# Windowed attention feeding a Fourier mixing block: dilated heads of batch 0 moved into the mixing tiles by one-hot products

## The chip, the cores and the metric

The kernel runs on one core of a Trainium2 chip. The metric is the device time of one execution in microseconds (us). Five things work side by side: TensorE (PE, matrix products), VectorE (DVE), ScalarE (ACT), GpSimd (POOL), and SyncE (SP), which here only issues DMAs. TensorE writes into PSUM, whose eight banks of 512 fp32 columns are handed out by name.

## The reference

All of it is fp32. Eight batches, eight heads, 576 tokens, head width 64, model width 512, hidden width 2048.

```python
scores = (q @ k^T) / 8                    # q, k, v: [8, 8, 576, 64]
rel = pos[:, None] - pos[None, :]
heads 0..3: keep 0 <= rel < 32            # "plain"
heads 4..7: keep 0 <= rel < 128, rel % 4 == 0   # "dilated"
attn = softmax(where(keep, scores, -1e9)); x = attn @ v   # x: [8, 576, 512]
u = x + real(fft(fft(x, axis=1), axis=2))
un = (u - mean(u)) / sqrt(var(u) + 1e-6)
out = u + relu(un @ w_ch1) @ w_ch2        # [512, 2048], [2048, 512]
```

## The kernel before

**Stages.** For each batch there are eight attention units (plain or dilated, `j` = pair of heads, `u` = first or second half of the tokens), then a mixing step, then the feed-forward net of that batch's tokens. Six of the sixteen hidden blocks of the net (`NF1 = 6`) are done in a first pass, called fill (`up`, L1104, and `down`, L1120), while attention and mixing of later batches still run; the other ten are done in a late stage (L1386, L1484, L1451) that follows.

**One attention unit** (`attend`): scores by products of 64 columns of weights on quarters of the array (L636), a mask with a row maximum on DVE (L667), `exp` on ACT (L673), transposes on PE (L687), a copy of the transposed probabilities out of PSUM on ACT (L692, L697), products with `v` on PE (L723), then sums, reciprocals and a scaled eviction on DVE (L733, L735, L746, L751). fp32 products appear as two instructions each in the trace; transposes as one. Dilated heads are computed with tokens regrouped by residue modulo 4, so that they too have a plain band.

**How batch 0 gets into the mixing.** The mixing folds token t with token 576 - t, so it wants rows 0 to 288 ("plus") in the tiles x0, x2, xt0 and the mirrored rows ("minus") in x1, x3, xt1. Batch 0 does its dilated heads first: they are evicted into `xt` and `xl`, stored to DRAM by `store` in pieces (segments of constant residue) that put the tokens in order, and fetched back by the first lines of `fold`. For batch 0 both ways go through POOL's DMA queue (`Q_ST0`, `Q_X0`; L543 for all of them). The plain heads of batch 0 are then written straight into the x tiles (L740). Their second half is `straight`: its products with `v` are made by `across` (L706 to L711) with 64 columns of weights, and at four places with one column of weights, one after the other in the order of a list. Later batches store and fetch both kinds through SP's queue.

**The mixing** (`mix`): `fold` (L873 to L898), products along the sequence with the tables `seq` (L924), products along the channels with the tables `chn` (L970, L976), the sum into the x tiles (`add_u`), layer norm (`normalise`), and for batch 0 transposes on PE (`turned`, L818) into the operand of the fill. In `mix` the products along channels run over the row groups 0, 2, 1, and layer norm and transposes of group 0 follow those of group 2.

**Feed-forward weights** arrive as fp64 words and are narrowed on ACT and DVE (`narrow`, L1045 to L1056), then split into a high and a low part (`two_parts`, L1062 to L1066). In the kernel before, the first six of the twelve weight tiles of the fill have their high part copied on POOL (L1062), the rest on ACT (L1064).

**The order of the work** is made by a planner (`Plan.run`) when the program is built: every operation has an engine, a cost, a priority (a number; smaller goes first) and its dependences, and a list scheduler with a model of the engines, the PE clock and the DMAs lays each engine's instructions out in one fixed order. On the chip each engine works that order off in sequence, so an instruction whose input is late holds all that stand behind it. The constants P_... are offsets in those priorities, T_SEQ and T_CHN are earliest times in the model for the issue of the tables `seq` and `chn` on POOL's queue, NGANG is the unit from which scores wait for the eviction of two units before, and NPT2 and NAV2 say how many units use two banks rather than one for transposes and for products with `v`; one of the two banks is lent by the fill (`ff`), whose first use waits until these units are done.

**Spin products.** Up to 250 pairs of products of a blank tile (L564) are put into the order wherever PE has nothing else to do; their result is not used. They are left out from the time the model has given out the first bank to the fill or the eleventh to the mixing.

Of the kernel before, what the change touches and what calls it, by code (L numbers as in the profile page):

```python
# [18 lines left out]
C, FF = 512, 2048  # L19
# [20 lines left out]
NPT2, NAV2 = 11, 11  # L40
NGANG = 6
NHP = 6
W_ON = (("POOL", "POOL"), ("POOL", "ACT"))
# [4 lines left out]
NFD, NUD, NFL = 1, 0, 1  # L48
# [7 lines left out]
Q_ST0, Q_X0 = 'P', 'P'  # L56
# [6 lines left out]
GAP = 32  # L63
DIL = 4
# [147 lines left out]
class Plan:  # L212
# [60 lines left out]
    def run(self):  # L273
# [164 lines left out]
def fused_kernel(ctx: ExitStack, tc, qk, v, w1, w2, seq, tail, chn, alt, mask, ident, perm, flip, out):  # L438
# [98 lines left out]

    def dma(fn, r, w, prio, nbytes, slow=1):
        return add("SP", 0.5, fn, r, w, prio, nbytes * slow)
# [7 lines left out]
    def start():  # L547
# [9 lines left out]
        for t in qks + lent[:1]:  # L557
            zero(t, "POOL", 0.1, lambda t=t: nc.gpsimd.memset(t()[:, GAP - WIN:GAP], 0.0), "z", -8.0)
        zero(blank, "DVE", 0.3, lambda: nc.vector.memset(blank().bitcast(F32), 0.0), None, -9.0)
        spin = Buf(ap=mixes[0][:, NSP:NSP + 220])  # L560
        for n in range(NSPIN):
            def turn_over(n=n):
                for k in range(2):
# [5 lines left out]
        for t, p, w in ((xs[1], 0, C // 2), (xtail[1], 32, C // 2)):  # L569
            zero(t, "DVE", 0.1, lambda t=t, p=p, w=w: nc.vector.memset(t()[p:p + 1, 0:w], 0.0), "row")  # L570
# [6 lines left out]
        for b in range(B):  # L577
# [5 lines left out]
    def tables_in():  # L583
        def table(dst, src, key, prio, nbytes):
            add("POOL", 0.55, lambda: nc.gpsimd.dma_start(out=dst(), in_=src), (), (key,), prio, nbytes, at=T_SEQ if prio == P_SEQ else T_CHN)
# [13 lines left out]
    def attention(b, when):  # L599
        for n, dil in enumerate((0, 1) if b else (1, 0)):  # L600
            xts = []
            if b or dil:
                xts = [attw("xt", [P, 2, 4, D], F32, NXT) for _ in range(2)] + [attw("xl", [P, 2, D], F32, 1)]
            for j in range(2):
                attend_pair(b, dil, j, 2 * n + j, xts, lambda u: when(6 * n + 3 * j + 1.5 * u))

# [16 lines left out]
    def attend(b, dil, j, u, num, qk_, vt, xts, prio):  # L623
# [55 lines left out]
        def order(m):  # L679
            if m == 4 or not dil and m == 3:  # L680
# [32 lines left out]
        def values():  # L713
            if straight:
                across(0)
                across(1)
# [36 lines left out]
        if j == 1:  # L753
            store(b, dil, u, xt, xl, prio)

# [86 lines left out]
    def mix(b, when):  # L842
# [10 lines left out]
        def fold(m, prio):  # L853
# [3 lines left out]
            if m < 2:  # L857
                xp, xm = tiles[m]
                at = slice(0, P)
                for x, src in ((xp, plus), (xm, minus)):  # L860
                    send("S" if b else Q_X0, lambda x=x: x()[:, cs], lambda src=src: src()[P * m:P * m + P, cs],
                         (src,), ((x, 0),), early, P * (2048 if b else 1024))
            else:
# [5 lines left out]
                ):  # L869
# [25 lines left out]
            either(b < NFL, NEH, lambda on: on.tensor_tensor(  # L895
                out=hl(1, 0), in0=ee()[:n], in1=hl(0, 0).bitcast(F32), op=ALU.subtract), (ee, eb), (eb,), prio)
            either(b < NFL, 2 * P, lambda on: on.tensor_tensor(
# [161 lines left out]
    def two_parts(src, need, dst, key, n, eng, prio, high="ACT"):  # L1059

        if high == "POOL":
# [513 lines left out]
```

## Time and profile before

| | us |
|---|---|
| median of 3 runs (range) | 1024.17 (1023.91 to 1027.3) |
| the profiled execution, whole | 1026.06 |
| its span, first to last instruction | 1024.3 |
| PE busy in the span | 1010.2 (99%) |
| of it, spin products (L564) | 37.1 |
| DVE, ACT, POOL busy | 730.9, 474.1, 291.5 |
| mean granted PE clock | 0.992 |

The profile is one execution; its own time is 1.89 us above the median. "Granted clock" is the share of TensorE's full speed: 1.00 is 2.4 GHz, 0.50 is 1.2 GHz. "PEld" is the loading of weights into the array, which overlaps the products. A row of a timeline gives start, duration, engine, source line, operation, output<-inputs and, in brackets, how long the engine stood idle before and what ended that. A PE that is busy with L564 does nothing useful.

### The profile page before, as it was taken

The numbers are of one execution on the slowest core, as the hardware profiler recorded it, in microseconds if no ns is written. First come the engines' busy times: TensorE is split into PE (matmuls) and PEld (weight loads), VectorE is DVE, ScalarE is ACT, GpSimd is POOL, SyncE is SP. The second block draws the span as 40 slices with busy tenths as digits, with TensorE's granted clock in tenths as the row PEclk, the third lists the DMA queues.
The fourth block names the chain that finished last, engine by engine and source line by source line (L and its number), as shares of the span: only waits on it lengthen the run. The fifth ranks groups of instructions, "written<-read, shape, count | busy, mean of one in ns | idle before, by whom it ended". The sixth has DMA issues, their size and how long they took to land.

```text
span 1024.3 us, 22200 instructions
## 1 busy us (share of the span) xinstructions
PE 1010.2 (99%) x8371; PEld 902.1 (88%) x8371; DVE 730.9 (71%) x2151; ACT 474.1 (46%) x1180; POOL 291.5 (28%) x353
## 2 busy tenths in 40 slices
PE   9999899999999999999999999999999999999998
PEld 8788688888988988899998898989898989898987
DVE  4489987878766687877575476858585858585846
ACT  5365756655645343434434443526252625262522
POOL 3536572536434557441321010101010101010200
PEclk9799999999999999999999999999999999999999
DMA  9867778786763545234354132323232323232221
GB/s 291 256 201 233 243 205 225 225 233 181 228 180 104 159 122 170 86 115 144 124 155 104 52 83 83 83 83 83 83 83 83 84 83 83 83 84 83 83 62 42
DMA packets 98875, 137.91 MB, mean 135 GB/s; under 512 B 9678, under 2 KB 62143, under 8 KB 98768
## 3 DMA queue, kind: packets, MB, share of 16 engines
q1 hardware_dynamic: 94112, 125.66, 42.1%
q0 software_dynamic: 4128, 9.71, 3.4%
q8 instruction: 66, 1.08, 0.5%
q10 hardware_dynamic: 528, 1.11, 0.3%
q14 instruction: 41, 0.34, 0.1%
HBM read 99.24 MB, written 37.21 MB: 133 GB/s over the span
## 4 chain that ended last, share of the span: by engine, by line
PE 88%; DVE 5%; DMA 4%; ACT 1%; issue 1%; SPq 0%; POOL 0%; DVEq 0%; ACTq 0%; POOLq 0%
PE bank L1386 24%; PE bank L1484 20%; PE bank L1120 13%; PE bank L1104 12%; PE bank L723 3%; PE bank L970 3%; PE bank L636 3%; PE bank L687 3%; PE bank L924 3%; DMA seq<-in_seq_dram 2%; PE bank L564 2%; PE bank L1451 1%; PE bank L709 1%; DVE pm L667 1%; DMA wst<-in_w_dram 1%
## 5 line engine op out<-in xcount | busy, mean ns | idle before, releaser
L1386 PE MATMUL bank<-low,wb 128*128 128x512 f32 x1080 | 255.6, 389 | 0.0
L1386 PEld LDWEIGHTS bank<-low,wb 128*128 128x128 f32 x1080 | 198.0, 188 | 36.9
L1104 PE MATMUL bank<-ut,low 128*128 128x256 f32 x1296 | 167.1, 282 | 0.8 <-DVE low L1112 0.8
L1104 PEld LDWEIGHTS bank<-ut,low 128*128 128x128 f32 x1296 | 157.1, 189 | 3.8 <-DVE low L1112 1.2
L1120 PE MATMUL bank<-low 128*128 128x512 f32 x648 | 156.4, 392 | 0.5 <-DVE low L1112 0.5
L1148 POOL DMA_INDIRECT ut<-us,flip_sb x20 | 41.7, 2083 | 393.2 <-DVE ut L1205 208.5
L1120 PEld LDWEIGHTS bank<-low 128*128 128x128 f32 x648 | 118.6, 188 | 23.8 <-DVE low L1112 0.7
L1392 ACT ACTIVATE xa<-bank 128x256 f32<-128x256 f32 x90 | 34.2, 380 | 176.6 <-PE bank L1386 176.6
L673 ACT ACTIVATE pm<-pm,mx 128x96 f32<-128x96 f32 x256 | 83.1, 369 | 55.4 <-DVE mx L667 54.4
L1423 DVE TENSOR_TENSOR y<-xa 128x384 f32<-128x384 f32 x45 | 25.1, 558 | 101.9 <-ACT xa L1392 101.6
L1112 DVE SCALAR_TENSOR_TENSOR low<-bank,low 128x256 fp32r<-128x256 f32 x108 | 45.2, 420 | 49.4 <-ACT low L1110 48.7
L1110 ACT ACTIVATE low<-bank 128x256 fp32r<-128x256 f32 x108 | 41.1, 382 | 72.9 <-PE bank L1104 72.2
L1194 DVE TENSOR_TENSOR ut<-ut,bank 128x512 f32<-128x512 f32 (+1 forms) x136 | 73.1, 547 | 2.1
L1227 DVE STREAM_TRANSPOSE ut<-ut 128x512 f32<-128x512 f32 (+1 forms) x76 | 70.2, 976 | 5.1 <-DMA ut<-us 5.0
L1484 PEld LDWEIGHTS bank<-w2s,low 128*128 128x128 f32 x588 | 71.7, 188 | 2.1
L1484 PE MATMUL bank<-w2s,low 128*128 128x256 f32 x588 | 72.1, 278 | 0.0
L667 DVE CUSTOM_DVE_ANT_0 pm<-bank,mask_sb 128x96 f32<-128x96 f32 x256 | 54.7, 249 | 18.6 <-PE bank L636 17.7
L1484 PEld LDWEIGHTS bank<-w2s,hm 128*128 128x128 f32 x483 | 58.9, 188 | 1.8
L1484 PE MATMUL bank<-w2s,hm 128*128 128x256 f32 x483 | 59.2, 278 | 0.0
L1140 ACT COPY row<-bank 128x512 f32<-128x512 f32 x36 | 21.1, 585 | 78.0 <-PE bank L1120 67.8
L1064 ACT CAST low<-y 128x640 fp32r<-128x640 f32 (+1 forms) x50 | 35.8, 716 | 41.2 <-DVE y L1425 23.9
L1484 PE MATMUL bank<-low 128*128 128x256 f32 x420 | 51.5, 278 | 0.0
(187 smaller groups left out, 1810.1 us busy)
## 6 DMA issues: line engine op xcount, KB each, us to landing
qk<-in_qk_dram SPq DMA_DIRECT2D x30, 576.0 KB
vt<-in_v_dram SPq DMA_DIRECT2D x31, 438.8 KB
us<-uc SPq DMA_DIRECT2D x36, 257.0 KB
part<-row SPq DMA_DIRECT2D x36, 256.0 KB
wst<-in_w_dram SPq DMA_DIRECT2D x18, 512.0 KB
ut<-us SPq DMA_DIRECT2D x36, 256.0 KB
ut<-part SPq DMA_DIRECT2D x36, 256.0 KB
ut<-us SPq DMA_DIRECT2D x64, 128.0 KB
```

The source lines that it names most:

```text
L667: nc.vector.tensor_tensor_reduce(prob(i)[ps_], sc()[e][ps_, KB * (i // 2):KB * (i // 2) + KB], mask_sb().bitcast(F32)[ps_, kind], -0.125, ...
L673: add("ACT", 0.265, lambda i=i: nc.scalar.activation(out=prob(i), in_=prob(i), func=AF.Exp, bias=mx()[:, i:i + 1], scale=-1.0), ((mx, i),) ...
L1064: add("ACT", act(n), lambda: nc.scalar.copy(out=dst(0), in_=src()), need, ((key[0], (key[1], 0)),), prio)
L1104: nc.tensor.matmul(z()[:, :n_tok], lhsT=wf()[a][:, kk], rhs=ut()[:, p, kk], start=(kk == 0 and n == 0), stop=(kk == KT - 1 and n == 2),)
L1110: add("ACT", act(n_tok) - 0.05, lambda: nc.scalar.activation(out=h()[:, 0, :n_tok], in_=z()[:, :n_tok], func=AF.Relu), (z,), ((h, 0),), prio)
L1112: add("DVE", dve(n_tok), lambda: nc.vector.scalar_tensor_tensor(h()[:, 1, :n_tok], z()[:, :n_tok], 0.0, h()[:, 0, :n_tok].bitcast(F32), op ...
L1120: nc.tensor.matmul(acc(), lhsT=h()[:, a, P * s:P * s + P], rhs=wf()[:, p], start=(first and n == 0), stop=(last and n == 2),)
L1148: add("POOL", 1.04, lambda: nc.gpsimd.indirect_dma_start(dst(), None, us[idx // 4](), bass.IndirectOffsetOnAxis(ap=flip_sb()[:, 4 * kk + i ...
L1194: add("DVE", dve(C if at in (outer, inner) else TOK1), lambda: nc.vector.tensor_tensor(out=blocks(part())[:, at], in0=blocks(part())[:, at ...
L1227: nc.vector.transpose(out=o[back], in_=x[:, g])
L1386: nc.tensor.matmul(z(), lhsT=wb1[NF1 + 2 * p + f]()[:, a, kk], rhs=ut()[:, x, kk], start=(kk == 0 and n == 0), stop=(kk == KT - 1 and n == 2),
L1484: nc.tensor.matmul(acc()[block // 2][:, TOK1 * (block % 2):TOK1 * (block % 2) + TOK1], lhsT=part(hl, a, i, i + 1), rhs=w2s[p]()[:, j, x], ...
```

## The change

- **Dilated heads of batch 0.** They no longer go through DRAM. A tile `comb` holds two identity patterns spread over every fourth column; slices of it are one-hot matrices. After each dilated unit, `settle` multiplies such slices with the evicted `xt` and `xl` (fp32) into a bank of PSUM called home, which puts the tokens in order and separates plus from minus; `settled` copies home into the x tiles (six copies of 256 columns on ACT, and one memset on POOL). There are three homes (row groups 0, 1, 2), taken from the two banks of the mixing. `store` and the fetch in `fold` are left out for batch 0, and so is the zero row of its `xsm`. The transposes of the dilated units of batch 0 use the plain identity instead of `perm`.
- **One-column products.** `across` issues all twelve products with 64 columns of weights of both heads first and the eight with one column last.
- **Order in `mix`.** The products along channels of all three row groups are listed before any layer norm and transposes; the banks of the mixing are given out in that order.
- **Spin products.** 32 columns instead of 220, into another bank, and left out only once the fill has its first bank.
- **Weights.** The high parts of all twelve weight tiles of the fill are copied on ACT.
- **Constants.** T_SEQ and T_CHN are gone, NPT2 and NAV2 go from 11 to 13, NGANG from 6 to 10, and all priority offsets differ. NFL is replaced by NFD of the same value; Q_ST0 and Q_X0 are no longer used.

```diff
-NPT2, NAV2 = 11, 11
-NGANG = 6
-NHP = 6
-W_ON = (("POOL", "POOL"), ("POOL", "ACT"))
+NPT2, NAV2 = 13, 13
+NGANG = 10
-P_QK0, P_V0 = -8.77, -8.57
-P_ST, P_FD, P_WD, P_ST0, P_FD0, P_SPAN0, P_SPAN1 = 6.01, -1.43, -0.9, -38.42, -6.42, 14.09, 37.25
-P_QK, P_V, P_TR, P_MIX, P_SPAN, P_W, P_WF, P_FILL, P_FILLT = 7.55, 24.08, -5.32, 2.19, 23.68, 14, 4.61, 45.36, 4.44
-P_MIX0, P_MIX1 = -4.08, -39.02
-P_SEQ, P_CHN = -11.04, -19.08
-T_SEQ, T_CHN = 4.31, 37.98
+P_QK0, P_V0 = -3.77, -0.7
+P_ST, P_FD, P_WD, P_ST0, P_FD0, P_SPAN0, P_SPAN1 = -9.42, -1.79, -5.67, -44.72, -26.2, -0.04, 23.28
+P_QK, P_V, P_TR, P_MIX, P_SPAN, P_W, P_WF, P_FILL, P_FILLT = 3.24, 3.62, -16.9, 1.77, 11.53, 21.01, 4.61, 39.84, 3.58
+P_MIX0, P_MIX1 = 8.6, -13.7
+P_SEQ, P_CHN = -30.6, 12.62
+P_HOME = 7.4
+BACK = 4 * P + 72
-            if o.prio == SPIN and (turn["ff"] or turn["mix"] > 10):
+            if o.prio == SPIN and turn["ff"]:
+    comb = work("y1", [P, 2, 2, NSP], F32R, 1)
+    def teeth(lo, n):
+        return comb().rearrange("p a c k -> p (a c k)").bitcast(F32)[:, lo:lo + n]
+        zero(comb, "DVE", 0.8, lambda: nc.vector.memset(teeth(0, 4 * NSP), 0.0), None, -9.0)
+        for k in range(2):
+            add("DVE", 0.2, lambda k=k: nc.vector.tensor_copy(
+                out=teeth(k * BACK, 4 * P)[:, ::4], in_=ident_sb().bitcast(F32)[:, k]), (ident_sb,), (comb,), -8.0)
-        spin = Buf(ap=mixes[0][:, NSP:NSP + 220])
+        spin = Buf(ap=pair[0][:, 5 * KB:512])
-                    nc.tensor.matmul(spin(), lhsT=blank(), rhs=blank().unsqueeze(1).broadcast_to([P, 2, P])[:, :, 0:110],
-                                     start=n + k == 0, stop=True, skip_group_check=True)
+                    nc.tensor.matmul(spin(), lhsT=blank(), rhs=blank()[:, 0:32], start=True, stop=True)
...
         def order(m):
+            if dil and not b:
+                return ident_sb().bitcast(F32)[:, 0], 0
...
-        def across(e):
-            for k, g, lo, n, t in ((0, 0, 0, QB, 8), (0, 1, 64, QB, 7), (0, 1, 64, 1, 8), (2, 0, 128, QB, 6), (2, 0, 128, 1, 7),
-                                   (2, 1, 192, QB, 5), (2, 1, 192, 1, 6), (4, 0, 256, QB, 4), (4, 0, 256, 1, 5), (4, 1, 289, QB, 4)):
+        def across():
+            for e, (k, g, lo, n, t) in itertools.chain(itertools.product(range(2), (
+                    (0, 0, 0, QB, 8), (0, 1, 64, QB, 7), (2, 0, 128, QB, 6), (2, 1, 192, QB, 5), (4, 0, 256, QB, 4), (4, 1, 289, QB, 4))),
+                    itertools.product(range(2), ((0, 1, 64, 1, 8), (2, 0, 128, 1, 7), (2, 1, 192, 1, 6), (4, 0, 256, 1, 5)))):
...
-        if j == 1:
+        if b and j == 1:
             store(b, dil, u, xt, xl, prio)
+    def settle(m, j, u, xts, home, prio):
+        xt, xl = xts[u], xts[2]
+        n = (P, P, 33)[m]
+        todo = [(0, r, P * r, xt, r % 2) for r in (2 * u, 2 * u + 1)]
+        rows = P if m < 2 else 32
+        for s_ in (2 * u, 2 * u + 1):
+            for r in range(4):
+                lo, hi = max(P * s_, 144 * r + (112, 80, 72)[m]), min(P * s_ + P, 144 * r + (144, 112 + (r == 0), 80 + (r == 0))[m])
+                if lo < hi:
+                    todo.append((1, r, P * s_, xt, s_ % 2))
+        if u and m < 2:
+            todo += [(1, 3, 4 * P - QB * e, xl, e) for e in range(2)]
+        def go(side_):
+            for k, (side, r, first, src, at) in enumerate(todo):
+                if side != side_:
+                    continue
+                off = 575 * r - 4 * first
+                lhs = teeth(BACK + 4 * P - 4 - (off + S - P * m), rows) if side else teeth(off + P * m, n)
+                o = home()[:rows if side else n, 256 * side:256 * side + 256].rearrange("p (e h d) -> p h e d", e=2, h=2)[:, j]
+                o, x = (o[:, at], src()[:, j]) if src is xl else (o, src()[:, at, j::2, :])
+                nc.tensor.matmul(o, lhsT=lhs, rhs=x, start=k == 0 and not j and not u, stop=True, skip_group_check=True)
+        for side in range(2):
+            add("PE", 0.215 * sum(t[0] == side for t in todo), lambda side=side: go(side), ((xt, j), comb) + ((xl, j),) * u * side, (home,), prio)
+    def settled(m, home, prio):
+        for side, x in enumerate(xtail if m == 2 else xs[2 * m:2 * m + 2]):
+            n = P if m < 2 else 33 - side
+            add("ACT", act(C // 2) - 0.05, lambda x=x, side=side, n=n: nc.scalar.copy(
+                out=x()[:n, C // 2:C], in_=home()[:n, 256 * side:256 * side + 256]), (home,), ((x, "dil"),), prio)
...
-                for x, src in ((xp, plus), (xm, minus)):
+                for x, src in ((xp, plus), (xm, minus)) if b else ():
...
         for n, m in enumerate((0, 2, 1)):
             along_channels(m, when(0.55 + 0.15 * n))
-            if n == 0:
-                continue
-            m = n - 1
+        for m in range(2):
```

## Rows read from the trace of the kernel before

**Rows 1.** The page's first part: busy us, share of span, instructions of each engine.
```profile
PE 1010.2 (99%) x8371; PEld 902.1 (88%) x8371; DVE 730.9 (71%) x2151; ACT 474.1 (46%) x1180; POOL 291.5 (28%) x353
```

**Rows 2.** By stage: length; PE, PEld, DVE, ACT, POOL busy; granted clock; DMA share; GB/s.
```profile
8.30:26.40 18.10, 16.98 (x304) 14.50 (x303) 11.48 (x95) 13.15 (x43) 4.33 (x10) 1.00 1.17 311
26.40:42.60 16.20, 16.16 (x125) 11.91 (x129) 6.62 (x26) 2.99 (x8) 7.75 (x17) 0.69 0.99 276
...
50.50:87.00 36.50, 34.98 (x462) 31.13 (x460) 32.12 (x138) 22.36 (x64) 17.82 (x21) 1.00 0.70 210
87.00:131.00 44.00, 39.65 (x510) 33.07 (x510) 41.33 (x174) 31.16 (x87) 22.39 (x25) 1.00 0.75 236
131.00:260.00 129.00, 128.31 (x1550) 110.47 (x1548) 102.55 (x491) 78.30 (x223) 65.32 (x92) 1.00 0.76 219
260.00:1024.30 764.30, 758.95 (x5297) 686.51 (x5289) 531.21 (x1190) 321.22 (x746) 165.79 (x169) 1.00 0.35 102
```

**Rows 3.** The same stretches, spin products (L564) alone.
```profile
8.30:26.40 18.10, 6.98 (x41) 5.53 (x40) 1.00 1.17 311
26.40:42.60 16.20, 5.10 (x20) 4.59 (x20) 0.69 0.99 276
...
50.50:87.00 36.50, 12.79 (x92) 11.04 (x90) 1.00 0.70 210
sum 86.00, PE 37.09 PEld 32.87; mean PE 7.42 PEld 6.57
```

**Rows 4.** The chain that ended last: start us, us, piece.
```profile
26.46 4.84 PE bank L709 x39
...
36.00 4.49 PE bank L709 x40
...
50.89 0.73 PE bank L723 x20
```

**Rows 5.** PE by half microseconds: stretch, length, PE busy, granted clock, DMA.
```profile
28.50:29.00 0.50, 0.50 (x10) 1.00 1.14 440
29.00:29.50 0.50, 0.50 (x4) 0.52 1.02 397
...
46.50:47.00 0.50, 0.50 (x7) 1.00 1.01 406
```

**Rows 6.** POOL's timeline: a table load, then the end of batch 0's dilated heads.
```profile
1.98 0.58 POOL L549 DMA_DIRECT2D ident_sb<-in_ident_dram  x1
...
25.77 0.51 POOL L543 DMA_DIRECT2D xsm<-xt  x1 [0.46 <-DMA seq<-in_seq_dram]
26.27 0.12 POOL L702 MEMSET ptsb<- 96x2 f32 x1
...
37.34 1.48 POOL L543 DMA_DIRECT2D xt<-xsm  x3
```

**Rows 7.** ACT's timeline: the copy before the first `across`.
```profile
24.19 0.26 ACT L697 COPY ptsb<-bank 96x128 f32<-96x128 f32 x1
```

**Rows 8.** DVE's timeline: first mask, last plain eviction of batch 0, first fold.
```profile
9.40 0.26 DVE L667 CUSTOM_DVE_ANT_0 pm<-bank,mask_sb 128x96 f32<-128x96 f32 x1 [6.36 <-PE bank L636]
...
42.06 0.58 DVE L740 TENSOR_TENSOR xt<-bank,rinv 32x128 f32<-32x128 f32 x2
...
49.10 0.16 DVE L733 TENSOR_SCALAR sums<-bank 128x4 f32<-128x4 f32 x1 [2.50 <-PE bank L723]
...
50.56 0.42 DVE L873 TENSOR_TENSOR t<-x,x 128x257 f32<-128x257 f32 x1
```

**Rows 9.** DMA issues of the first 120 us: queue, count, KB, us to landing.
```profile
x<-xsm POOLq DMA_DIRECT2D x2, 128.0 KB, 5.9
...
ident_sb<-in_ident_dram POOLq DMA_DIRECT2D x1, 192.0 KB, 9.9
```

**Rows 10.** Groups by line: a copy out of PSUM on ACT; high parts on POOL.
```profile
L980 ACT COPY pc<-bank 128x258 f32<-128x258 f32 x16 | 5.9, 371 | 2.0 <-PE bank L976 2.0
...
L1062 POOL CAST low<-ut 128x512 fp32r<-128x512 f32 x6 | 3.9, 645 | 21.7 <-DVE ut L1054 21.7
```

More of the change, by code (lines that the diff above doesn't have):

```diff
@@ L1 @@
 import heapq
+import itertools
 from contextlib import ExitStack
@@ L576, in start @@
         zero(ye, "DVE", 0.2, lambda: nc.vector.memset(ye().bitcast(F32), 0.0))
-        for b in range(B):
+        for b in range(1, B):
             dma(lambda b=b: nc.sync.dma_start(
@@ L584, in table @@
         def table(dst, src, key, prio, nbytes):
-            add("POOL", 0.55, lambda: nc.gpsimd.dma_start(out=dst(), in_=src), (), (key,), prio, nbytes, at=T_SEQ if prio == P_SEQ else T_CHN)
+            add("POOL", 0.55, lambda: nc.gpsimd.dma_start(out=dst(), in_=src), (), (key,), prio, nbytes)
         for i in range(2):
@@ L603, in attention @@
                 xts = [attw("xt", [P, 2, 4, D], F32, NXT) for _ in range(2)] + [attw("xl", [P, 2, D], F32, 1)]
+            homes = [bank("mix") for _ in range(2)] if not b and dil else []
             for j in range(2):
                 attend_pair(b, dil, j, 2 * n + j, xts, lambda u: when(6 * n + 3 * j + 1.5 * u))
+                if not b and dil:
+                    for u in range(2):
+                        for m in range(2):
+                            settle(m, j, u, xts, homes[m], when(6 * n + 3 * j + 1.5 * u) + P_HOME)
+            if not b and dil:
+                for m in range(2):
+                    settled(m, homes[m], when(6 * n + 4.5) + P_HOME)
+                home = bank("mix")
+                for j in range(2):
+                    for u in range(2):
+                        settle(2, j, u, xts, home, when(6 * n + 4.5) + P_HOME)
+                settled(2, home, when(6 * n + 4.5) + P_HOME)
     def attend_pair(b, dil, j, at, xts, when):
@@ L714, in values @@
             if straight:
-                across(0)
-                across(1)
+                across()
                 return
@@ L1003, in mix @@
             along_channels(m, when(0.55 + 0.15 * n))
-            if n == 0:
-                continue
-            m = n - 1
+        for m in range(2):
             idx = 4 * b + 2 * m
@@ L1057, in narrow, with two_parts @@
         return lambda: shaped(bits(F32))
-    def two_parts(src, need, dst, key, n, eng, prio, high="ACT"):
-        if high == "POOL":
-            add("POOL", pool(n), lambda: nc.gpsimd.tensor_copy(out=dst(0), in_=src()), need, ((key[0], (key[1], 0)),), prio)
-        else:
-            add("ACT", act(n), lambda: nc.scalar.copy(out=dst(0), in_=src()), need, ((key[0], (key[1], 0)),), prio)
+    def two_parts(src, need, dst, key, n, eng, prio):
+        add("ACT", act(n), lambda: nc.scalar.copy(out=dst(0), in_=src()), need, ((key[0], (key[1], 0)),), prio)
         lo = nc.gpsimd if eng == "POOL" else nc.vector
@@ L1068, in two_parts, with prep, prep_up @@
             (*need, (key[0], (key[1], 0))), ((key[0], (key[1], 1)),), prio)
-    def prep(rows, three, dst, t, gate, prio, eng="POOL", high="ACT"):
+    def prep(rows, three, dst, t, gate, prio, eng="POOL"):
         x = narrow(rows, three, t, gate, prio)
-        two_parts(x, ((t, "bits"),), lambda i: dst()[i] if isinstance(dst(), list) else dst()[:, i], (dst, "w"), C, eng, prio, high)
-    def prep_up(f, dst, t, gate, prio, eng="POOL", high="ACT"):
-        prep(w1.rearrange("(j k) f -> j k f", k=KT)[:, :, P * f:P * f + P], True, dst, t, gate, prio, eng, high)
+        two_parts(x, ((t, "bits"),), lambda i: dst()[i] if isinstance(dst(), list) else dst()[:, i], (dst, "w"), C, eng, prio)
+    def prep_up(f, dst, t, gate, prio, eng="POOL"):
+        prep(w1.rearrange("(j k) f -> j k f", k=KT)[:, :, P * f:P * f + P], True, dst, t, gate, prio, eng)
     def prep_pair(f, dst, stage, gate, behind, prio, eng):
```

22 lines of the change are left out of this document (12 added, 10 removed).

## The prediction

> **What bounds the kernel now.** I read the page's first part, then busy time by stage, then the spin products by the same stages, then the chain and the single engines of the first 90 us.
>
> PE is busy for 1010.2 of 1024.3 us [rows 1], but 37.1 of these are spin products [rows 3], so useful PE work is 973.1 us and PE is without it for 51.2 us (37.1 of spins, 14.1 idle). Where these lie is what the reader should see. From 131 us on PE is full: 128.31 of 129.0 us, then 758.95 of 764.3 [rows 2], with no spins. The end is therefore set by how much useful PE work is left when PE first becomes full, near 131 us, and by when that is.
>
> Before that, three stretches differ. From 8.3 to 42.6 us batch 0's attention runs, and nobody is full: DVE is busy for 11.48 of 18.1 and 6.62 of 16.2 us, ACT for 13.15 and 2.99, and PE spins for 6.98 and 5.10 [rows 2, 3]. It is a stretch of latencies. From 50.5 to 131 us DVE is the bound: 32.12 of 36.5 and 41.33 of 44.0 us, with masks, folds, evictions and the narrowing of weights, while PE still spins for 12.79 us and then idles for 4.35 [rows 2, 3]. So an edit that lets DVE start on its long list earlier moves everything behind it; an edit that only gives PE less to do between 50 and 131 us moves little.
>
> What holds DVE back between 26 and 50 us? The two `across` pieces of the chain, 4.84 and 4.49 us [rows 4], with DVE waiting for their sums; then, from the last plain eviction (42.06 + 0.58 = 42.64 us) to the first fold at 50.56 us, 7.92 us [rows 8].
>
> **The change part by part.** The sum is made on the profiled execution (span 1024.3 us, 1026.06 us whole, 1.89 us above the median); as a difference it is then taken from the median, 1024.17 us.
>
> *One-column products.* The trace shows 39 instructions in 4.84 us, 124 ns each, with the granted clock still 1.00 up to 29.0 us; the ordinary products with `v`, of the same 65 columns, take 0.73 us for 20, 36.5 ns each [rows 4, 5]. The clock doesn't explain the first half of that factor of 3.4; the mixture of 64 and 1 columns of weights is the visible difference. In the old list the width changes eight times per head, sixteen times per call; in the new one once. Taking the 24 wide instructions at 36.5 ns (0.88 us) and the 16 narrow ones between 36.5 and 124 ns (0.58 to 1.98 us), a call costs 1.5 to 2.9 us; I take 2.0. Two calls save 4.84 + 4.49 - 4.0 = 5.3 us (3.6 to 6.4; nothing, if the width isn't the cause), all on DVE's path. The Trainium skill (TensorEngine Tiling, Tiling Modes) says that a change of tiling mode, not just of tile, drains TensorE. The trace agrees: (4.84 - 40 x 0.0365) / 16 gives 0.21 us per change of width, an estimate.
>
> *POOL's queue.* The memset before the first `across` runs at 26.27 us, behind POOL's store at 25.77, though ACT's copy that it follows was done at 24.45 (24.19 + 0.26) [rows 6, 7]. Without batch 0's stores that is 1.8 us earlier. Nothing else on POOL then is late; its table loads are issued ahead. Gain 1.8 us (0 to 1.8).
>
> *Stores and fetches of batch 0.* Fetches end their issue at 37.34 + 1.48 = 38.82 us and land some 5.9 us after issue [rows 6, 9], near 44.7 us, 2 us after the plain heads are ready. The other 6 us up to the fold are DVE's own fixed order: masks of batch 1 stand ahead and wait, the last at 49.10 for products with `v` [rows 8]. The changed program has no transfer for the planner to leave room for, but other offsets, so masks may stand there again. Gain between 0 and 7.9 us; I take 5.
>
> *Settle.* From the loops: 24 products to the plus side and 32 to the minus side, 48 of 128 columns and 8 of 64, each two instructions. No such product is in the trace. The nearest row is the product with `v`: 36.5 ns per instruction of 65 columns where two halves of the array work side by side, so at most 73 ns alone [rows 4]. For 128 columns and two instructions that is 0.14 to 0.29 us. I take 0.25, near the upper end, since a full-width product shares the array with none. Sum: 48 x 0.25 + 8 x 0.125 = 13 us (7.5 to 15). Cover: spins of 6.98 + 5.10 = 12.1 us in batch 0's stage [rows 3], less the 7.1 us by which the stage was just shortened, leaves 5. The 16 products of the third group (4 us) can run while DVE folds the first. So 13 - 5 - 4 = 4 us lie on the path (0, if all is hidden, to 13). The copies out of home are six of about 0.37 us [rows 10] on an ACT that is idle then; the first two delay the fold by 0.7 us.
>
> *Identity instead of `perm`, and `comb`.* DVE's tooth copies and PE's first transposes now wait for `ident`, which was issued at 1.98 us and landed 9.9 us after [rows 6, 9], at 11.9; the first mask ran at 9.40 us [rows 8]. If the copies stand before the masks, all of batch 0 starts up to 2.5 us later, and ACT and PE queue behind. I take 1.
>
> *Edits at nothing.* High parts of six weight tiles go from POOL (0.645 us each) to ACT, which copies half as many columns in 0.371 us [rows 10]; at 0.645 each as a bound that is 3.9 us more on an ACT that is busy for 22.36 of 36.5 us, then 31.16 of 44.0 [rows 2]; if that cover fails, 3.9 us. The tables `chn`, no longer held back, may join the first loads, while the DMA share is over 1 [rows 2]: their 1.19 MB (four of 128 x 516 fp32 and one of 128 x 258) at 311 GB/s are 3.8 us, against the 1.18 MB (576 x 256 fp32, twice) that batch 0 no longer stores and fetches; 0, from -4 to +4. Products along channels ahead of the first transposes put 12 products and their evictions ahead of the first fill, but the second fill comes earlier, and DVE's list is the same: 0 (-1 to +2). The two more units on double banks hold the first fill back only if it comes before unit 12; at 87 us it was long past that: 0. The new offsets reorder everything between 50 and 131 us; DVE's total there stays, so 0, with an unknown of some 5 us to either side.
>
> Sum: -5.3 - 1.8 - 5 + 4 + 0.7 + 1 = -6.4 us. DVE's list starts earlier by that, PE is full earlier by that, and what PE has left then is the same. 1024.17 - 6.4 = **1017.8 us**. With all favourable ends it would be about 1005.
>
> **The rivals.**
>
> *The order takes it back.* The round trip is gone but DVE's order isn't better: the fold stands behind waiting masks again (5 us lost). For it: 6 of the 7.9 us weren't the transfer. Against it: the fold now depends on nothing outside the core. -6.4 + 5 gives **1022.8 us**; with settle's full 13 us in the open it reaches 1032.
>
> *The narrow spins don't hold the clock (slower).* Place: 8 to 87 us. Today the granted clock falls from 1.00 (2.4 GHz) to 0.52 at 29.0 us after 2.5 us of `across`, and is back at 1.00 by 46.5 us, after spins of 220 columns had filled the gaps [rows 5]. With 32 columns nothing may bring it back before the work itself is dense. Price: useful PE work between 50.5 and 87 us is 34.98 - 12.79 = 22.2 us [rows 2, 3]; at 1.2 GHz it is 44.4 in a stretch of 36.5, 7.9 us more; and settle's 13 us become 26, of which I count half of the excess, 6.5, against a saving of 6.4 that then about cancels it. Together 1024.17 + 7.9 = **1032 us**, up to 1040 if batch 0's latencies double as well. It decides once the clock stands at 1.2 GHz for over half of 8 to 87 us. Against it: from 87 to 131 us there are no spins, PE idles a tenth, and the clock stays 1.00 [rows 2]; and settle's own products are wide. The skill (TensorE: Matmul & The Clock Gate, Part 1) says that the throttled state is the default and activity releases it, which speaks against narrower spins; what share of activity a 32-column spin gives, no row shows.
>
> *The reorder does nothing.* If `across` keeps its 124 ns, -6.4 + 5.3 gives **1023 us**. Against it stands the factor of 3.4 at full clock.
>
> **How the numbers follow.** About 0.5%, 5.1 us, is what a measurement of this kernel can tell from no change, so faster means below 1019.05 and slower above 1029.3. Forecast 0.50 (faster 0.46, same 0.04); the order takes it back 0.22 (faster 0.02, same 0.16, slower 0.04); the clock 0.20 (same 0.01, slower 0.19); no effect of the reorder 0.08 (faster 0.01, same 0.06, slower 0.01). That makes faster 0.49, same 0.27, slower 0.24. The range runs from 1005, all favourable ends, to 1034, which leaves out the far end of the clock's case. Faster and slower together hold most of the chance; the forecast's own range is 1007 to 1020.
>
> **What the profile would show.** Each `across` in 2.0 us, not 4.5 to 4.8. No POOL stores between 20 and 39 us. Settle's 56 products, 112 instructions, summing to some 13 us, most of them where spins were. The first fold near 44 us, not 50.56; the first fill near 80 us, not 87; PE without useful work for some 37 us, not 51, with useful work up by about 8. Wrong would be: granted clock at 0.50 for long before 87 us; the first mask at 12 us; DVE idle before the fold while home has long been copied; or a first fill as early as I say and PE idle behind it for longer than 4.35 us.

## The result, and the profile after

The changed kernel takes 1031.01 us (1029.84 to 1034.38), the one before 1024.43 us (1021.85 to 1028.06) on the same chip: a ratio of 1.0062, 95% interval 1.0042 to 1.0082. It is slower by some 6.4 us. The profiled execution has a span of 1029.4 us.

The page's first part after the change, to be held against [rows 1]:

```profile
PE 1014.5 (99%) x8401; PEld 908.1 (88%) x8401; DVE 736.0 (72%) x2154; ACT 477.2 (46%) x1192; POOL 277.2 (27%) x327
```

The stages of [rows 2] after the change (length; PE, PEld, DVE, ACT, POOL busy; granted clock; DMA share; GB/s):

```profile
8.30:26.40 18.10, 16.87 (x152) 14.43 (x154) 4.91 (x41) 7.24 (x22) 2.16 (x4) 1.00 1.18 328
26.40:42.60 16.20, 16.20 (x260) 14.58 (x257) 8.95 (x64) 8.05 (x25) 0.31 (x4) 1.00 0.85 254
...
50.50:87.00 36.50, 35.23 (x508) 30.17 (x507) 33.93 (x159) 28.10 (x81) 10.29 (x11) 1.00 0.66 195
87.00:131.00 44.00, 41.99 (x509) 35.76 (x508) 37.38 (x170) 28.27 (x79) 22.90 (x28) 0.92 0.76 232
```

The spin products alone (now L573), answering [rows 3]:

```profile
1.00:8.30 7.30, 6.03 (x29) 6.03 (x29) 1.00 0.91 297
8.30:26.40 18.10, 7.44 (x31) 6.97 (x31) 1.00 1.18 328
...
50.50:87.00 36.50, 6.72 (x48) 6.04 (x48) 1.00 0.66 195
87.00:131.00 44.00, 5.68 (x36) 5.35 (x36) 0.92 0.76 232
sum 130.00, PE 25.87 PEld 24.39; mean PE 4.31 PEld 4.07
```

In the first stage PE is as busy as before (16.87 against 16.98 us) but issues 152 products in place of 304, and DVE is busy for 4.91 us, not 11.48: batch 0's attention gets less than half as far in this stretch. Useful PE work is 1014.5 - 25.9 = 988.6 us, 15.5 more than before; part of that is the same work taking longer at a lower clock. PE is without useful work for 1029.4 - 988.6 = 40.8 us.

PE's timeline: the first spins, the first scores, both `across`, settle's last group, the first fill.

```profile
2.27 10.00 PE L573 MATMUL bank<-blank 128*128 128x32 f32 x46 [2.27 <-DVE blank L568]
12.20 1.88 PE L657 MATMUL bank<-qk 64*64 64x96 f32 x36
...
18.94 1.24 PE L657 MATMUL bank<-qk 64*64 64x96 f32 x20 [0.27 <-DVE mx L688]
...
39.24 1.47 PE L733 MATMUL bank<-vt,ptsb 96*64 96x65 f32 x40
...
44.62 1.47 PE L733 MATMUL bank<-ut,ptsb 96*64 96x65 f32 x40
...
48.49 4.51 PE L800 MATMUL bank<-xt,y 128*33 128x128 f32 x32
...
97.62 1.63 PE L1155 MATMUL bank<-ut,low 128*128 128x256 f32 x6
```

The same lines of before, for the first two and the last:

```profile
1.05 7.33 PE L564 MATMUL bank<-blank 128*128 128x220 f32 x46 [1.05 <-DVE blank L559]
8.31 1.06 PE L636 MATMUL bank<-qk 64*64 64x96 f32 x36
...
86.93 0.60 PE L1104 MATMUL bank<-ut,low 128*128 128x256 f32 x3
```

DVE's timeline, answering [rows 8]: the last plain eviction of batch 0 and the first fold.

```profile
47.04 0.57 DVE L763 TENSOR_TENSOR xt<-bank,rinv 32x128 f32<-32x128 f32 x2
49.25 0.42 DVE L929 TENSOR_TENSOR t<-x,x 128x257 f32<-128x257 f32 x1
```

The first scores run 3.9 us later than before and take 1.88 us in place of 1.06. The column of the granted clock reads 1.00 there in both kernels, so this rests on durations: the column reads 1.00 up to the first change that a profile records, whatever the clock was before it. Run 8 below has such products where the column does read 0.50. Plain evictions end 5.0 us later (47.61 against 42.64), the first fold still comes 1.3 us earlier, and the first fill 10.7 us later (97.62 against 86.93).

### The profile page after: what moved, and what is told of

It reads as the page before. It is cut to its first block, busy times and chain, and to the rows that moved or that the text cites. A ratio compares the mean times of both kernels' runs of the same rounds, so it can differ in the third digit from the quotient of the medians.

```text
span 1029.4 us, 22216 instructions
## 1 busy us (share of the span) xinstructions
PE 1014.5 (99%) x8401; PEld 908.1 (88%) x8401; DVE 736.0 (72%) x2154; ACT 477.2 (46%) x1192; POOL 277.2 (27%) x327
## 4 chain that ended last, share of the span: by engine, by line
PE 91%; DVE 5%; issue 1%; ACT 1%; POOL 0%; DMA 0%; SPq 0%; DVEq 0%; ACTq 0%
PE bank L1437 24%; PE bank L1535 20%; PE bank L1155 13%; PE bank L1171 13%; PE bank L1026 3%; PE bank L746 3%; PE bank L657 3%; PE bank L710 3%; PE bank L980 3%; PE bank L573 2%; PE bank L800 1%; PE bank L1502 1%; DVE pm L688 1%; PE bank L1002 1%; DMA ut<-us 0%
## 5 line engine op out<-in xcount | busy, mean ns | idle before, releaser
L1155 PE MATMUL bank<-ut,low 128*128 128x256 f32 x1296 | 170.1, 284 | 1.1 <-DVE r L864 0.8
L1115 ACT CAST low<-y 128x640 fp32r<-128x640 f32 (+1 forms) x50 | 35.8, 716 | 41.3 <-DVE y L1476 24.0
```

The lines of the kernel that those rows point to most:

```text
L1115: add("ACT", act(n), lambda: nc.scalar.copy(out=dst(0), in_=src()), need, ((key[0], (key[1], 0)),), prio)
L1155: nc.tensor.matmul(z()[:, :n_tok], lhsT=wf()[a][:, kk], rhs=ut()[:, p, kk], start=(kk == 0 and n == 0), stop=(kk == KT - 1 and n == 2),)
```

## The experiments

Two theories stood at first. **Spins:** the narrow ones leave TensorE's clock at its lower level, or stand in PE's fixed order ahead of work that is ready. **Order:** settle's products and the new offsets cost more than the shorter `across` and the missing round trip bring. Ratios are against the kernel before, measured beside each: runs 1 to 4, 5 to 8 and 9 to 12 stood on three chips, where it took 1025.86, 1024.66 and 1025.63 us. Differences between runs are of medians.

**Run 1, e1_wide_spins.** The changed kernel; up to the first settle product its spins are 220 columns wide, later ones as in the change.

```diff
+early = Buf(ap=mixes[0][:, 0:220])
...
+if before_settle[0]:
+    nc.tensor.matmul(early(), lhsT=blank(), rhs=blank().unsqueeze(1).broadcast_to([P, 2, P])[:, :, 0:110], start=True, stop=True)
+else:
     nc.tensor.matmul(spin(), lhsT=blank(), rhs=blank()[:, 0:32], start=True, stop=True)
```

> The changed kernel in the same order, but every spin product ahead of the first settle product streams 220 columns instead of 32 and goes into a bank of the mixing. Clock theory (narrow spins leave TensorE at 1.2 GHz to about 29 us, and the 46 spins ahead of the first scores then take 10.0 us instead of 7.3): first scores near 8.5 us instead of 12.2, their 36 instructions in 1.06 us instead of 1.88, last plain eviction of batch 0 near 39 us instead of 47.6, time 1023 to 1026 us. Order theory (the new priorities and settle's work cost the time, whatever the clock): scores earlier, but first fill within 3 us of 97.6 us and time 1028 to 1031 us.

Measured: 1022.87 us, ratio 0.9968 [0.9952, 0.9983]. The clock is up at 8.4 us: from there on a spin takes some 0.13 us, before it 0.22. The last two rows are DVE's first fold and PE's first fill.

```profile
2.27 8.32 PE L576 MATMUL bank<-blank 128*128 128x220 f32 x46 [2.27 <-DVE blank L569]
10.52 1.05 PE L662 MATMUL bank<-qk 64*64 64x96 f32 x36
...
40.08 0.42 DVE L935 TENSOR_TENSOR t<-x,x 128x257 f32<-128x257 f32 x1
...
89.79 1.63 PE L1161 MATMUL bank<-ut,low 128*128 128x256 f32 x6
```

**Run 2, e2_spin_bank.** As run 1, but 32 columns wide, so that only the PSUM bank differs from the change.

```diff
-early = Buf(ap=mixes[0][:, 0:220])
+early = Buf(ap=mixes[0][:, 0:32])
...
-nc.tensor.matmul(early(), lhsT=blank(), rhs=blank().unsqueeze(1).broadcast_to([P, 2, P])[:, :, 0:110], start=True, stop=True)
+nc.tensor.matmul(early(), lhsT=blank(), rhs=blank()[:, 0:32], start=True, stop=True)
```

> As the run with wide spins, but 32 columns are kept: only the bank of the spins ahead of the first settle product changes, so that masks no longer wait for spins. Clock theory: TensorE slow to about 29 us as before, first scores at 12.2 us, time within 2 us of the changed kernel (1029 to 1032 us). Bank theory (the waits of masks for spins in their own bank, 3.6 us in all, delay batch 0): time 1026 to 1028 us.

Measured: 1030.5 us, ratio 1.0053 [1.0034, 1.0072]; by durations the clock is up at 29.0 us.

```profile
2.27 9.99 PE L576 MATMUL bank<-blank 128*128 128x32 f32 x46 [2.27 <-DVE blank L569]
12.19 1.88 PE L662 MATMUL bank<-qk 64*64 64x96 f32 x36
```

Runs 1 and 2 have the same instructions in the same order and differ in one width: 7.6 us. The bank is nothing. And the narrow spin isn't even short: the 48 of the stretch from 50.5 to 87 us take 6.72 us, 140 ns each; before, 92 wide ones took 12.79 us there, 139 ns [rows 3].

**Run 3, e3_no_spins.** The changed kernel in the same order, no spin issued.

```diff
-for _ in range(2):
-    nc.tensor.matmul(spin(), lhsT=blank(), rhs=blank()[:, 0:32], start=True, stop=True)
+pass
```

> The changed kernel in the same order with no spin product at all (they compute nothing that is used). Clock theory: narrow spins raise no clock, so without them the first scores start when their operands land, near 8 us instead of 12.2, still at half speed to about 25 us; time 1026 to 1029 us. If narrow spins do help the clock: slower than the changed kernel, 1033 us or more.

Measured: 1018.31 us, ratio 0.9929 [0.9906, 0.9951]: faster than both kernels, and than either theory said. Its first scores wait for their operands alone; by durations the clock rises at 19.7 us, shortly behind settle's first products. With narrow spins it rose at 29.5 us: later than with none.

```profile
5.67 1.88 PE L656 MATMUL bank<-qk 64*64 64x96 f32 x36 [5.67 <-DMA qk<-in_qk_dram]
...
12.40 0.92 PE L656 MATMUL bank<-qk 64*64 64x96 f32 x16 [0.32 <-issue]
...
18.52 1.06 PE L799 MATMUL bank<-xt,y 128*128 128x128 f32 x4
...
20.32 0.56 PE L656 MATMUL bank<-qk 64*64 64x96 f32 x16
...
41.52 0.42 DVE L928 TENSOR_TENSOR t<-x,x 128x257 f32<-128x257 f32 x1
...
85.62 1.70 PE L1154 MATMUL bank<-ut,low 128*128 128x256 f32 x6
```

So the spins cost 1031.0 - 1018.3 = 12.7 us, in two parts: 7.6 us are the width of those ahead of settle (run 2 against run 1), 4.6 us the rest (run 1 against run 3); the bank makes the 0.5 us left over, which is within the measurement. For the rest, run 1 is ahead of run 3 at the first fold (40.08 against 41.52 us), thanks to the earlier clock, and behind it at the first fill (89.79 against 85.62), 5.6 us lost between the two. There 10.90 us of its remaining narrow spins, from 50.5 to 87 us, stand ahead of work in PE's order; its clock is also at 0.50 from 84 to 92 us, against 0.57 from 84 to 88 in run 3. Run 8, without spins behind settle, needs 44.5 us from fold to fill, run 3 44.1, run 1 49.7.

**Run 4, e4_before_narrow.** The kernel before with spins of 32 columns.

```diff
-rhs=blank().unsqueeze(1).broadcast_to([P, 2, P])[:, :, 0:110]
+rhs=blank()[:, 0:32]
```

> The kernel before with 32 columns in its spins instead of 220, same bank, same order, nothing else. Clock theory: first scores near 12 us instead of 8.3, TensorE at 1.2 GHz to beyond 40 us since no settle products raise the clock, time 1031 to 1037 us. Order theory: the spins are not what costs, time 1024 to 1027 us.

Measured: 1044.38 us, ratio 1.0213 [1.0139, 1.0286]. First scores at 10.98 us, clock up at 26.6 us and down again from 43.7 to 67.6 us and from 71 to 81 us. That is some 19 us, beyond the 1031 to 1037 expected: in the kernel before, narrow spins do more harm than in the change.

**Run 5, e5_before_reorder.** The kernel before with the new order of the one-column products alone.

```diff
-across(0)
-across(1)
+across()      # 24 wide instructions, then 16 narrow ones
```

> The kernel before with one thing changed: the new order of the one-column products (24 wide instructions, then 16 narrow ones), spins and everything else as before. Theory: each of the two calls drops from 4.84 and 4.49 us to the 1.47 us seen in the changed kernel, DVE's sums come 6.4 us earlier in all, and as DVE is the bound from 50 to 131 us, nearly all of it reaches the end: -4 to -6.4 us, some 1018 to 1020. The granted clock no longer falls at 29 us. Rival 1: the gain stops at the fold, which waits for the stores and fetches of batch 0 (first fold still at 50 us or so): -0 to -2 us. Rival 2: the 124 ns of an instruction were the falling clock and not the change of width: then the calls stay over 3 us.

Measured: 1025.42 us, ratio 1.0011 [0.9995, 1.0027]: no change (rival 1), though each `across` takes 1.47 us and the last plain eviction ends at 34.83, not 42.64 us. POOL's queue and DVE's first fold (start, us, instruction, idle time before it):

```profile
34.64 1.11 POOL L544 DMA_DIRECT2D x<-xsp  x2 [4.17 <-DMA xsp<-xt]
```

```profile
48.07 0.43 DVE L874 TENSOR_TENSOR t<-x,x 128x257 f32<-128x257 f32 x1 [8.27 <-DMA x<-xsm]
```

DVE is early and waits 8.27 us for the round trip. The fetches go out when they did before (34.64 against 34.56 us), because POOL waits for the stores to land, and the fetch of `x` from `xsm` now takes 12.1 us to land, not 5.9 [rows 9], in a stretch (42.6 to 50.5 us) whose DMA share is 1.06 against 0.62. Of 7.8 us at the last plain eviction 2.5 are left at the first fold and 0.6 at the first fill (86.35 against 86.93). What eats these last is not shown; while PE stands idle for the round trip, its granted clock falls, to 0.50 from 46.6 to 56.8 us, where before it reads 1.00 from 46.5 us on.

```profile
42.60:50.50 7.90, 1.33 (x16) 0.85 (x17) 2.43 (x11) 1.08 (x5) 3.18 (x6) 0.75 1.06 230
```

**Run 6, e6_few_settle.** Run 3 with 12 of settle's 56 products.

```diff
-if side != side_:
+if side != side_ or u or any(t[0] == side for t in todo[:k]):
```

> The changed kernel without any spin, and with 12 of the 56 products that bring the dilated heads into x: the first of each side for the first pair of positions, the others are left out, so that the mixing of batch 0 reads sums that are not complete. It prices these products by themselves. At 0.28 us for one of 128 columns (15.8 us for all 56 in the changed kernel) some 12 us of PE work are gone. Theory A (they are in the open, since nothing else is ready then and PE is full later): 8 to 12 us less than the run without spins, some 1006 to 1010. Theory B (they lie in time that PE spends waiting anyway, between batch 0's attention and the first fold): under 4 us less, 1014 to 1018. A second reading: with fewer of them the clock may rise later than 19.7 us, which would take back 1 to 3 us.

Measured: 1014.94 us, ratio 0.991 [0.9875, 0.9945]; 3.4 us below run 3 by the medians, 1.9 by the ratios, and the intervals overlap. The first fill comes at 80.66, not 85.62 us. About 12 us of products bring at most 3.4: theory B. The clock is already up here, by durations, at the first settle product: its two instructions take 0.39 us at 18.00 us, as at 26.70.

**Run 7, e7_mix_earlier.** Run 3 with the old offset for batch 0's mixing.

```diff
-P_MIX0, P_MIX1 = 8.6, -13.7
+P_MIX0, P_MIX1 = -4.08, -13.7
```

> The changed kernel without any spin, with one number of the planner set back to that of the kernel before: the offset of batch 0's mixing, -4.08 in place of 8.6, so that its folds and evictions stand further ahead of the attention of batches 1 and 2 in the engines' order. Theory (the 12 us between first fold and first fill that the new offsets added are lost at the start of PE's full time): first fill 6 to 10 us earlier than at 85.6 us, and 2 to 6 us less in all, 1012 to 1016. Rival: DVE's list up to 131 us is the same in any order, so the first fill comes earlier and PE idles behind it by as much: within 2 us of the run without spins. A third way: PE's fixed order then stands behind a mixing that is not ready, and it gets slower by 2 to 5 us.

Measured: 1027.86 us, ratio 1.0016 [0.9995, 1.0037]: 9.5 us slower than run 3, more than any theory said. The first fill is earlier by 1.1 us only (84.54). What follows later costs more (PE by stretches: length, busy, granted clock):

```profile
136.00:140.00 4.00, 3.10 (x38) 0.74 0.93 338
140.00:144.00 4.00, 3.36 (x35) 0.50 0.38 97
144.00:148.00 4.00, 3.05 (x36) 0.50 0.00 0
148.00:152.00 4.00, 3.33 (x26) 0.50 0.50 163
```

Here attention runs almost alone (instructions from 136 to 152 us: 72 of scores, 16 transposes, 36 with `v`, only 4 of 512 columns), PE has gaps, and the clock falls. In run 3 the same 16 us hold 72 instructions of a fill, PE is full and the clock is 1.00. The clock isn't all of it: the two of its ten executions with a mean granted clock of 0.995 and 0.997 took 1023.8 us, the five with 0.988, the profiled one among them, 1027.9 to 1028.6. So some 4 of the 9.5 us go with the falls of the clock; the other 5.5 are there without most of them.

**Run 8, e8_early_wide_spins.** The change with 30 spins of 220 columns, all before the first settle product, 18 of them ahead of the first scores.

```diff
-    nc.tensor.matmul(spin(), lhsT=blank(), rhs=blank()[:, 0:32], start=True, stop=True)
+    if before_settle[0] and count[0] > 14:
+        nc.tensor.matmul(early(), lhsT=blank(), rhs=blank().unsqueeze(1).broadcast_to([P, 2, P])[:, :, 0:110], start=True, stop=True)
```

> The changed kernel in the same order of work, with spins only where nothing else can run: none of the first 28, then products of 220 columns up to the first product that brings dilated heads into x, none after that. Theory: width holds the clock (full from about 12 us on at the latest, not from 29.5 us), and a spin costs only where it stands ahead of work that is ready; so first scores below 9 us and 1014 to 1018 us, at or below the run without any spin (1018.3). Rival: the run without spins already raises its clock by its own products at 19.7 us, and spins in a fixed order displace as much as the clock gives back: 1018 to 1022.

Measured: 1021.17 us, ratio 0.996 [0.994, 0.998]; the rival by the median. The ten executions part in two: four of 1017.5 to 1019.3 us with a mean granted clock of 0.994 to 0.997, six of 1021.0 to 1023.5 us with 0.990 to 0.993, the profiled one among these. A transpose of 0.28 us at 11.40 us, where one at the lower clock takes 0.45 (17.56 us), shows the clock up; it falls at once, behind a stretch in which PE waits for the masks and the identity (1.02 us busy from 8 to 10 us, 0.60 from 10 to 12):

```profile
10.00:12.00 2.00, 0.60 (x4) 0.98 1.18 371
12.00:16.00 4.00, 3.40 (x43) 0.50 1.12 335
...
20.00:24.00 4.00, 4.00 (x86) 1.00 1.21 315
```

```profile
14.34 1.24 PE L662 MATMUL bank<-qk 64*64 64x96 f32 x20 [0.26 <-DVE mx L693]
...
23.54 0.73 PE L662 MATMUL bank<-qk 64*64 64x96 f32 x20
```

These rows also date the clock of the changed kernel: 20 scores take 1.24 us at a granted clock of 0.50 and 0.73 us at 1.00. After the change they take 1.24 us at 18.94 us.

**Run 9, e9_no_round_trip.** Run 5 without batch 0's stores and fetches.

```diff
-if j == 1:
+if j == 1 and (b or not dil):
     store(b, dil, u, xt, xl, prio)
-for x, src in ((xp, plus), (xm, minus)):
+for x, src in ((xp, plus), (xm, minus)) if b else ():
```

> The kernel before with the new order of the one-column products, and without the stores and fetches of batch 0's dilated heads: their half of x is set to zero at the start, so that part of the computation is left out and nothing stands in for it (no settle products). With the stores and fetches, the same order left DVE 8.27 us of waiting for the fetch of x before its first fold at 48.07 us, and brought nothing in all. Theory (the two parts gain only together): first fold at some 40 us, 5 to 8 us less than with the round trip, 1017 to 1020. Rival: what ends the stretch up to 131 us is DVE's list or the weights, and an earlier fold is waited for elsewhere: first fill still near 86 us, 1023 to 1026.

Measured: 1022.11 us, ratio 0.9976 [0.9955, 0.9996]; 3.3 us less than run 5. DVE's first fold and PE's first fill:

```profile
35.19 0.42 DVE L876 TENSOR_TENSOR t<-x,x 128x257 f32<-128x257 f32 x1
```

```profile
76.33 1.31 PE L1107 MATMUL bank<-ut,low 128*128 128x256 f32 x9
```

The fold is 12.9 us earlier and the first fill 10.0 us, yet the end only 3.3: PE then idles 5.87 us from 87 to 131 us (38.13 busy of 44.0; run 5: 3.98), and the clock falls behind a gap (0.67 from 100 to 104 us). Neither theory was right; of the 10.0 us at the first fill a third arrives. Part even of this third may be the low clock of run 5 from 46.6 to 56.8 us: over the whole profiled execution the granted clock is 0.998 here and 0.993 in run 5.

**Run 10, e10_old_order_no_spins.** Run 3 with the one-column products in the old order.

```diff
-across()
+across(0)
+across(1)
```

> The changed kernel without any spin, and with the one-column products in the old order (two calls of 4.84 and 4.49 us before, 1.47 us each now). Here no store or fetch stands between these products and the first fold. Theory: the 6.4 us come back in full on DVE's path, first fold 6 us later than at 41.5 us, 1022 to 1025 against 1018.3. Rival: they are hidden here too, behind settle's products, which PE has to finish ahead of the fold in any case: within 2 us of 1018.3.

Measured: 1024.56 us, ratio 0.9991 [0.997, 1.0011]: 6.2 us more than run 3, as the theory said. First fold at 46.71, first fill at 91.35 us.

```profile
31.02 4.10 PE L731 MATMUL bank<-vt,ptsb 96*64 96x65 f32 x39
...
38.95 4.31 PE L731 MATMUL bank<-ut,ptsb 96*64 96x65 f32 x40
```

```profile
31.00:34.50 3.50, 3.50 (x37) 1.00 1.05 253
34.50:39.00 4.50, 4.50 (x53) 1.00 1.04 228
```

The first of these calls lies wholly in a stretch of granted clock 1.00: it is the changes of width that cost, 105 ns per instruction against 37. The clock doesn't fall in either call here, as it did at 29.0 us before [rows 5], so the slow calls alone don't bring that about.

**Run 11, e11_before_no_spins.** The kernel before with no spin issued.

```diff
-for k in range(2):
-    nc.tensor.matmul(spin(), lhsT=blank(), ...)
+pass
```

> The kernel before with no spin issued at all, its order of work kept. It tells whether spins of 220 columns gain anything there. Theory A (before, nothing else is dense enough ahead of the first mixing to raise the clock, so without spins batch 0's attention runs at half speed): slower by 5 to 15 us, 1030 to 1040; with narrow spins it was 20 us slower, of which the rest is what the narrow spins displace. Theory B (as in the changed kernel, spins displace as much as they give): within 3 us of before, or faster by up to 6.

Measured: 1027.13 us, ratio 1.0021 [0.9999, 1.0044]. The clock stands at 0.50 for all of 42.6 to 50.5 us, and still the medians differ by 1.5 us, within the measurement: theory B. Early on, with attention alone on PE, no spin and no settle product, the clock is up by 23.3 us; at 16.30 us, where 20 products with `v` take 1.35 us, it isn't yet:

```profile
16.30 1.35 PE L721 MATMUL bank<-vt,ptsb 96*64 96x65 f32 x20 [0.18 <-ACT ptsb L695]
...
23.28 0.80 PE L721 MATMUL bank<-vt,ptsb 96*64 96x65 f32 x20
```

Wide spins hold the clock better in the kernel before and take about as much as they give.

**Run 12, e12_mix_loop_order.** Run 3 with the old order of issue inside the mixing.

```diff
-for m in range(2):
+    if n == 0:
+        continue
+    m = n - 1
```

> The changed kernel without any spin, with the old order of issue inside the mixing of a batch: normalising and turning two row blocks between the products along channels, not behind all of them. The prediction put this move at nothing (-1 to +2 us). Theory: within 2 us of 1018.3. Rival: the order of the mixing is worth more than that, because PE's gaps decide where the clock falls: then over 3 us to either side, with a fall of the granted clock between 60 and 160 us that the run without spins doesn't have.

Measured: 1021.54 us, ratio 0.9963 [0.9948, 0.9977]: 3.2 us more than run 3, the rival's side, though the two intervals just overlap. As in run 7, a sparse stretch comes with a fall of the clock that run 3 doesn't have:

```profile
140.00:144.00 4.00, 1.78 (x18) 0.67 0.84 238
144.00:148.00 4.00, 4.00 (x15) 0.50 0.65 219
```

That fall isn't all of it. The first fill already comes at 88.80 us, 3.2 later than in run 3, though the first fold is 0.6 earlier. And the profiled execution is the slowest of the ten (0.993 in the mean): six others have a mean granted clock of 0.997, that of run 3's profiled one (1019.86 us), and took 1020.7 to 1022.3 us.

## Why the prediction was wrong

It said 1017.8 us, with slower at 0.24. **The step that failed is the price of the narrow spins:** they stood in a rival at 0.20 and nowhere in the sum. Without them the change comes to 1018.31 us (run 3), by the ratio 7.3 us below the kernel before, where 6.4 were forecast; with them 12.7 us are lost. That 1018.31 lies so near 1017.8 is luck in part, as the terms below show: some came out smaller than said, and two that the sum put at nothing brought gains.

The rival's 1032 us is near the result, but not by its own working: it put the half clock between 50.5 and 87 us, where the rows read 1.00. The clock was low from the start to 29.5 us and again from 94 to 101 us, which is 21.5 of the 79 us from 8 to 87 where the rival asked for over half, and the spins that stand in PE's order behind settle cost 4.6 us more (runs 1 and 3). My argument against it, that settle's products are wide, doesn't help: 46 spins stand in front of the first scores, whose operands land at 5.67 us, and the clock was low through all of them. Nor is it settle that raises the clock. In run 6 the first settle product finds it up, and in run 11 it rises with no such product at all. What the runs show is that narrow spins keep it low longer than no spins do, to 29.5 us against 19.7 in the changed order and to 26.6 against 23.3 in the kernel before (run 4 and run 11). The Trainium skill (TensorE: Matmul & The Clock Gate, Part 1) says that the default is the throttled clock and that activity releases it. Runs 1 and 2 agree that the start is slow, 8.4 us against 29.0 with the same instructions at two widths; they show besides that 46 products of 32 columns, back to back in 10 us, didn't release it.

By the other steps:
- **One-column products:** 1.47 us a call, not 2.0, and 6.2 us in the end (run 10) against 5.3 said. Right, with one thing missed: in the kernel before, alone, it is worth nothing (run 5), where the round trip is then the next to be late. I had counted the two as independent terms.
- **POOL's queue:** said 1.8, hardly there. With the stores gone (run 9) the first `across` starts at 26.22 us, with them (run 5) at 26.75.
- **Round trip:** said 5, measured 3.3 with the new order of the one-column products (run 9 against run 5), although the fold moved by 12.9. The sentence that DVE's list starts earlier and PE is full earlier by the same is what failed here: PE became short of work between 87 and 131 us.
- **Settle:** said 13 us of PE work with 4 on the path. It was 15.8 us at 0.14 us for an instruction of 128 columns where the clock is full (48.49: 32 in 4.51 us), at half clock more; at most 3.4 us of it counts for 44 of the 56 products (run 6).
- **Identity in place of `perm`:** the wait is there (in run 3 the first transposes wait 3.90 us for it, until 11.45 us). Its price alone wasn't measured. The sign of being wrong was there, a first mask at 14.11 us, but through the spins: in run 3 it comes at 9.30.
- **Edits at nothing:** two weren't nothing. The new order inside the mixing is worth 3.2 us (run 12), and the new offset of batch 0's mixing 9.5 us (run 7), both as gains. In both runs the clock falls between 136 and 152 us, for which I had no row, but run 12's first fill is 3.2 us late already, and of run 7's some 4 us go with the clock. From the later first fill I had first taken the new offsets for a loss; run 7 refuted that. The weights on ACT, the tables, the double banks and the other offsets weren't run alone.
- **The terms don't add up:** `across`, the order in the mixing and the one offset come to 18.9 us, each put back alone in run 3, while run 3 as a whole is 8.8 us below the kernel before without spins (run 11).

Expected marks: `across` at full speed and no stores on POOL were right; a fold near 44 us was wrong with spins (49.25) and near with none (41.52), a first fill near 80 us wrong in both (97.62 and 85.62). PE was without useful work for 40.8 us, not 37, with useful work up by 15.5, not 8. The last sign of being wrong, an early fill and PE idle behind it for longer than 4.35 us, is what run 9 shows (76.33 and 5.87). Open is what makes up the 5.5 us of run 7 that don't go with the clock, and run 12's 3.2; in runs 7, 9 and 12 the order of other work moves with the edit as well. The prediction's reading of the clock before left out that it was back at 1.00 from 35.8 to 39.3 us, between the two falls.

## What to carry to other kernels

A filler product has two prices, the clock that it does or doesn't hold and the ready work that it stands ahead of in a fixed order: measure the kernel without any filler before tuning the filler's shape. When two latencies lie one behind the other, as the slow products and the round trip did, the gain at one can be lost at the other: the same reorder brought nothing with the round trip behind it and 6.2 us without. And an earlier start of a stage is worth only as much as the engine behind it can use: look at the busy share and the granted clock of the next stretches, not at the first instruction alone.

## What the runs showed of the hardware

- Back-to-back products of 32 columns, 46 in 10.00 us with weight loads of 128 columns beside them, left the clock at its lower level (1.2 GHz): the first scores behind them took 1.88 us (run 2). Behind 46 of 220 columns, in 8.32 us, it was at 2.4 GHz, and the same scores took 1.05 us (run 1).
- A 32-column spin takes as long as one of 220: 140 and 139 ns, in the stretch from 50.5 to 87 us.
- Changing the width of the weights between one and 64 columns costs about 0.2 us each time at a granted clock of 1.00, an estimate from run 10: (4.10 - 39 x 0.0368) / 15 changes, the new list having one change where the old has sixteen.
- In run 7 the granted clock fell at 138 us, with PE busy for 1.60 of 2 us from 134 us and 0.49 of 1 us from 136 us, and it stayed at 0.50 up to 152 us while PE was busy for 3.05 to 3.36 of every 4 us.
- Ahead of the first recorded change the column of the granted clock reads 1.00 even at the lower level: 20 scores took 1.24 us at 18.94 us after the change, as long as at a recorded 0.50 in run 8, and 0.73 us at a recorded 1.00.
